# Moving the dense stretch of a weight conversion twelve steps earlier in a fused attention and expert kernel

## The chip, the cores and the metric

The kernel runs on one core of one Trainium2 chip. The metric is the device time of one execution in microseconds (us); lower is better. Engines are called by the profile's short names: PE (TensorE, matrix products; PEld is its weight load), DVE (VectorE), ACT (ScalarE), POOL (GpSimd) and SP (SyncE, which here only issues DMAs, in order).

## The reference

Three stages follow each other on 4 batches of 576 tokens. The kernel gets the inputs of the first two in 64-bit words, so weights have to be turned into 32-bit numbers on the chip.

```python
# 1: attention, 32 heads (4 batches x 8) of 576 x 64, with a decay bias from a running sum of s
cum = np.cumsum(np.maximum(s, 0.0), axis=-1)
bias = -(cum[:, :, :, None] - cum[:, :, None, :])
scores = np.where(causal, -1e9, scale * (q @ k^T) + np.minimum(bias, 0.0))
x = softmax(scores) @ v                       # heads joined: 4 x 576 x 512
# 2: token mixing of rank 32, and a feed-forward net 512 -> 2048 -> 512
u = x + ((x^T @ U) @ V)^T
y = u + np.maximum(u @ w_ch1, 0.0) @ w_ch2
# 3: four single-head attentions on y, the best two per token mixed by a gate
```

## The kernel before, in words

**Steps.** The first attention is written as a loop of steps `i`, five per head (one per block of query rows), 160 for 32 heads. A head pair `p` (two heads) takes ten steps, from step 10 x p. Instructions stand in each engine's queue in the order in which the loop writes them; no scheduler moves them. A step writes: the products `qk` of step i on PE (L361, L362), transposes `t` of the step ten before (L402, L405), the row minimum on DVE (L372), the exponential of step i-1 on ACT (L379), copies of the transposes out of PSUM, at a head's end the scaling of its rows on POOL (L390), a share of the product with V (`pv`, L429), and then what `fillers(i)` adds.

**Fillers.** `fillers(i)` adds, in this order: the preparation of the next pair (`prep_steps`: POOL and DVE split q and k into a high and a low part, and DMAs of L626 place them in the tiles `L`, `R`, `HI`, five pieces spread over six steps that end six steps before the pair starts); some slots of the weight conversion; and background work.

**Conversion.** One job converts a piece of 128 x 256 numbers. It is a load of 256 KB (`c_raw`, L186, issued on SP three jobs ahead), two passes on ACT (L116, L119), three on DVE (L122, L126, L130), and for the weight blocks f = 0, 1 and 2 a rounded high part on ACT (`wh`, L197) and the rest on POOL (`wl`, L200). A block f is four jobs. 24 jobs are converted in this loop: one of U, three of V, and four for each of f = 0 to 4. The list `STREAM` deals a job's parts over six slots, overlapped with its neighbours', and a step takes one slot or two:

```python
for _ in range(CONVS[FAST[0] < i < FAST[1]][i % NT]):   # CONVS: 1 a step, or 2 in the dense stretch
    if i >= 4 and convs:
        convs.pop(0)()
for _ in range(BG[i % NT]):                             # BG = (1, 1, 0, 2, 1)
    background()
```

**Background.** Once a batch's attention is done, its token mixing (`mx`, `mt`, `mo`: L236, L248, L259) and then the first three blocks of its feed-forward net are queued as small tasks. The net of one batch is 14 tasks: for each of two chunks of 288 tokens three `hps` (L293, 12 products, one per block f = 0, 1, 2) and four `facc` (L307, 9 products). A task `hps` of block f is taken only when that block is converted:

```python
ffn = ffnq and full.get(ffnq[0][0]) == 2 * DM
if mixq and (turn[0] % 2 or not ffn) and not (mixq[0][1] and ffnq):
    mixq.pop(0)[0]()
elif ffn:
    ffnq.pop(0)[1]()
```

This happens for batches 0, 1 and 2 inside the loop. After the loop come the other blocks of the net (L1010, L1028) and the last stage.

Of the kernel before, what the change touches and what calls it, by code (L numbers as in the profile page):

```python
# [50 lines left out]

PLAIN = (((0, 0),), ((0, 1),), ((0, 2), (1, -2)), ((1, -1),), ((2, -3),), ((0, 3),), ((0, 4),))
STREAM = (((0, 0), (3, -3)), ((-1, 4),), ((0, 1),), ((0, 2), (1, -2)), ((1, -1),), ((0, 3),))
FAST = (40, 70)
RAWS = 4

ENGA = ('vaaaaa', 'aavaav')
# [101 lines left out]
def fused_kernel(ctx, tc, qk, v, s, u, vv, w12, wp, out):  # L159
# [524 lines left out]
    with ExitStack() as cx:  # L684
# [228 lines left out]
        def fillers(i):  # L913
# [8 lines left out]
            for x in todo.pop(i, ()):  # L922
                x()
            for _ in range(CONVS[FAST[0] < i < FAST[1]][i % NT]):
                if i >= 4 and convs:
# [471 lines left out]
```

## Time and profile before

| what | value |
|---|---|
| time, median of 3 runs | 842.06 us (840.68 to 843.66) |
| the profiled execution: time / span | 842.4 us / 840.6 us |
| PE, PEld busy | 95%, 88% of the span |
| DVE, ACT, POOL busy | 63%, 56%, 38% of the span |
| granted clock of TensorE | 1.00 |

A product's end is modelled in the trace and products overlap, so that a busy PE is not PE at its peak. The span runs from the first to the last instruction; the time lies 1.8 us above it.

### The profile page before, as it was taken

What the parts mean: (1) busy time and instruction counts of PE and PEld (TensorE: products, weight loads), DVE (VectorE), ACT (ScalarE), POOL (GpSimd) and SP (SyncE); (2) the same over time, 40 slices, a digit from 0 to 9 for tenths busy, and PEclk for the clock granted to TensorE, in tenths of its full rate; (3) what the DMA queues carried; (4) which work ended last, traced back from release to release, by engine and by line L of the source; (5) the groups of instructions that cost most, each with busy time, mean ns of one, the idle gap of its engine ahead of it and who ended that gap; (6) DMA issues with size and microseconds to landing.
All of it is one profiled execution on the core that took longest, in us unless ns stands there. A gap on an engine that the chain in (4) does not pass through costs nothing.

```text
span 840.6 us, 17207 instructions
## 1 busy us (share of the span) xinstructions
PE 799.4 (95%) x6028; PEld 740.3 (88%) x6028; DVE 526.0 (63%) x1559; ACT 473.8 (56%) x1406; POOL 322.0 (38%) x483
## 2 busy tenths in 40 slices
PE   3889999999999899999999999999999989999997
PEld 2767779889888799999999999999999989898875
DVE  7779987776775357646554764455456775756541
ACT  5779996666776444434444442443334566655662
POOL 5647664453452334223322432232343043322231
PEclk9999999999999999999999999999999999999999
DMA  7887785745741342112111221210000111111221
GB/s 212 216 228 191 212 219 159 202 127 144 190 117 44 106 146 61 51 27 51 51 51 34 69 64 38 52 39 26 1 1 9 36 33 40 48 52 39 76 66 62
DMA packets 37048, 75.44 MB, mean 90 GB/s; under 512 B 4712, under 2 KB 8296, under 8 KB 36932
## 3 DMA queue, kind: packets, MB, share of 16 engines
q1 hardware_dynamic: 36964, 74.36, 32.5%
q8 instruction: 48, 0.79, 0.4%
q14 instruction: 36, 0.29, 0.1%
HBM read 38.93 MB, written 8.55 MB: 56 GB/s over the span
## 4 chain that ended last, share of the span: by engine, by line
PE 79%; DVE 10%; ACT 5%; DMA 3%; issue 2%; SPq 0%; POOL 0%; ACTq 0%; POOLq 0%; DVEq 0%
PE hps L1010 21%; PE facc L1028 21%; PE pv L429 4%; PE qkp L1237 4%; PE facc L307 3%; PE pv L589 3%; PE ops L1264 3%; PE hps L293 3%; PE t L402 3%; PE t L560 2%; PE vps L1171 2%; PE qk L361 2%; PE qk L362 2%; PE t L405 1%; DVE P L372 1%
## 5 line engine op out<-in xcount | busy, mean ns | idle before, releaser
L277 POOL TENSOR_TENSOR ul<-uT,uh 128x288 fp32r<-128x288 f32 x117 | 94.5, 828 | 163.9 <-ACT uh L276 138.1
L1015 DVE SCALAR_TENSOR_TENSOR hl<-hps,hh 128x288 fp32r<-128x288 f32 x110 | 50.3, 457 | 150.1 <-ACT hh L1014 150.1
L390 POOL TENSOR_SCALAR P<-P,stat 64x64 f32<-64x64 f32 (+4 forms) x160 | 101.7, 651 | 104.3 <-DVE stat L385 44.6
L1014 ACT ACTIVATE hh<-hps 128x288 fp32r<-128x288 f32 x110 | 45.0, 409 | 147.9 <-PE hps L1010 147.7
L85 ACT ACTIVATE pt<-t 64x64 f32<-64x64 f32 (+5 forms) x272 | 89.5, 358 | 42.0 <-PE t L405 29.6
L1010 PE MATMUL hps<-uh,wl 128*128 128x288 f32 x376 | 111.2, 296 | 0.0
L1010 PE MATMUL hps<-ul,wh 128*128 128x288 f32 x376 | 111.1, 296 | 0.0
L1028 PE MATMUL facc<-hh,wh 128*128 128x288 f32 x376 | 111.1, 296 | 0.0
L1010 PE MATMUL hps<-uh,wh 128*128 128x288 f32 x376 | 111.0, 295 | 0.0
L1028 PE MATMUL facc<-hh,wl 128*128 128x288 f32 x376 | 110.9, 295 | 0.0
L1028 PE MATMUL facc<-hl,wh 128*128 128x288 f32 x376 | 110.8, 295 | 0.0
L379 ACT ACTIVATE P<-P,stat 64x64 f32<-64x64 f32 (+4 forms) x160 | 89.2, 558 | 23.2 <-DVE stat L372 21.2
L548 POOL TENSOR_SCALAR P<-P,stat,pt 128x128 f32<-128x128 f32 (+4 forms) x72 | 45.8, 653 | 118.1 <-DVE stat L543 54.1
L372 DVE CUSTOM_DVE_ANT_0 P<-qk,mask 64x64 f32<-64x64 f32 (+4 forms) x160 | 77.4, 484 | 13.7 <-PE t L405 8.7
L361 PE MATMUL qk<-R,L 128*128 128x64 f32 (+2 forms) x192 | 66.3, 349 | 18.3 <-DVE L L750 9.6
L200 POOL TENSOR_TENSOR wl<-c_a_w,wh 128x256 fp32r<-128x256 f32 x56 | 43.8, 784 | 73.2 <-ACT wh L197 70.6
L1010 PEld LDWEIGHTS hps<-uh,wl 128*128 128x128 f32 x376 | 70.9, 189 | 0.0
L1028 PEld LDWEIGHTS facc<-hh,wl 128*128 128x128 f32 x376 | 70.9, 188 | 0.0
L1010 PEld LDWEIGHTS hps<-ul,wh 128*128 128x128 f32 x376 | 70.8, 188 | 0.0
L1028 PEld LDWEIGHTS facc<-hl,wh 128*128 128x128 f32 x376 | 70.8, 188 | 0.0
L1028 PEld LDWEIGHTS facc<-hh,wh 128*128 128x128 f32 x376 | 70.6, 188 | 0.1
L1010 PEld LDWEIGHTS hps<-uh,wh 128*128 128x128 f32 x376 | 70.6, 188 | 0.0
(211 smaller groups left out, 2230.0 us busy)
## 6 DMA issues: line engine op xcount, KB each, us to landing
c_raw_w<-in_w_dram SPq DMA_DIRECT2D x64, 256.0 KB
uT<-in_qk_dram SPq DMA_DIRECT2D x15, 576.0 KB
L<-HI SPq DMA_DIRECT2D x28, 288.0 KB
V<-in_v_dram SPq DMA_DIRECT2D x16, 320.0 KB
R<-HI SPq DMA_DIRECT2D x14, 288.0 KB
R<-uT SPq DMA_DIRECT2D x14, 288.0 KB
L<-uT SPq DMA_DIRECT2D x14, 288.0 KB
aD<-stage SPq DMA_DIRECT2D x6, 576.0 KB
```

The costliest lines, as they stand in the source:

```text
L85: nc.scalar.activation(out=out, in_=in_, func=AF.Copy)
L200: eng.tensor_tensor(out=wl, in0=t, in1=wh.bitcast(F32), op=OP.subtract)
L277: eng.tensor_tensor(out=l_, in0=src, in1=h_.bitcast(F32), op=OP.subtract)
L361: nc.tensor.matmul(ps[:, bk, :w], lhsT=q1[:, rows], rhs=k1[:, c0:c0 + w], start=True, stop=False)
L372: nc.vector.tensor_tensor_reduce(out=po, in0=view, in1=mk, scale=-self.scale, scalar=3.0e38, op0=OP.add, op1=OP.min, accum_out=stat[P - M: ...
L379: nc.scalar.activation(out=po, in_=po, func=AF.Exp, scale=-1.0, bias=stat[P - M:, 0, t:t + 1], accum_out=stat[P - M:, 1, t:t + 1])
L390: nc.gpsimd.tensor_scalar(out=pv, in0=pv, scalar1=stat[r0:, 2, t:t + 1], scalar2=1.0 if gate is None else gate(t)[r0:], op0=OP.mult, op1=O ...
L548: nc.gpsimd.tensor_scalar(out=po, in0=po, scalar1=stat[:, 2, s:s + 1], scalar2=1.0 if gate is None else gate(t), op0=OP.mult, op1=OP.mult)
L1010: nc.tensor.matmul(ps, lhsT=w[:, 0, cs], rhs=x, start=i == 0, stop=i == 11)
L1014: nc.scalar.activation(out=hh, in_=ps, func=AF.Relu)
L1015: nc.vector.scalar_tensor_tensor(out=hl, in0=ps, scalar=0.0, in1=hh.bitcast(F32), op0=OP.max, op1=OP.subtract)
L1028: nc.tensor.matmul(accs[c][d], lhsT=w[:, 1, cs], rhs=x, start=f == fs[0] and i == 0, stop=f == fs[-1] and i == 2)
```

## The change

One line: the dense stretch, in which a step takes two conversion slots, goes from steps 41 to 69 to steps 29 to 65. It is 37 steps long in place of 29.

```diff
 PLAIN = (((0, 0),), ((0, 1),), ((0, 2), (1, -2)), ((1, -1),), ((2, -3),), ((0, 3),), ((0, 4),))
 STREAM = (((0, 0), (3, -3)), ((-1, 4),), ((0, 1),), ((0, 2), (1, -2)), ((1, -1),), ((0, 3),))
-FAST = (40, 70)
+FAST = (28, 66)
 RAWS = 4
```

Counted from the code: steps 29 to 40 take 12 slots more, steps 66 to 69 take 4 less, and the stream, which is 8 slots ahead from there, ends at step 111 in place of 119. The last part of a block's conversion moves from step 47 to 41 (f = 0), 59 to 53 (f = 1), 73 to 65 (f = 2), 97 to 89 (f = 3) and 119 to 111 (f = 4).

Three places show what moves. The first is DVE's queue in step 30 and after, where head 6 starts (`qk_0` is its first block, `c_a_w` a piece of weights). Before:

```order
L87 COPY pt_106<-t_0_623 64x2x64
L849 TENSOR_TENSOR V_81<-c_a_v_547,V_81 128x192
L372 ISA P_114,stat_108<-qk_1_641,mask 128x192
L372 ISA stat_108 128x1
L384 TENSOR_SCALAR stat_112<-stat_112 128x5
L385 RECIPROCAL stat_112<-stat_112 128x5
L667 TENSOR_TENSOR uT<-uT,HI 128x576
L126 TENSOR_SCALAR c_a_w_0_666<-pt_106 128x256
L372 ISA P_114,stat_108<-qk_2_668,mask 128x320
L372 ISA stat_108 128x1
L667 TENSOR_TENSOR uT<-uT,HI 128x576
L130 ISA c_a_w_0_666<-c_a_w_0_666,pt_105 128x512
```

The same place with the change:

```order
L87 COPY pt_106<-t_0_624 64x2x64
L126 TENSOR_SCALAR c_a_w_0_641<-pt_106 128x256
L130 ISA c_a_w_0_641<-c_a_w_0_641,pt_105 128x512
L372 ISA P_114,stat_108<-qk_1_645,mask 128x192
L372 ISA stat_108 128x1
L384 TENSOR_SCALAR stat_112<-stat_112 128x5
L385 RECIPROCAL stat_112<-stat_112 128x5
L667 TENSOR_TENSOR uT<-uT,HI 128x576
L372 ISA P_114,stat_108<-qk_2_675,mask 128x320
L372 ISA stat_108 128x1
L667 TENSOR_TENSOR uT<-uT,HI 128x576
L122 SCALAR_TENSOR_TENSOR pt_105<-pt_107,c_r_w_256_670 128x256
```

The passes of the first piece (L126, L130) stand one and two steps earlier, and the first pass of the second piece (L122) has come into the row. The second place is SP's queue, where the tiles of pair 4 are placed in steps 29 to 34, before:

```order
L626 DMA L_0_122<-HI 64x1152
L626 DMA L_0_119<-HI 64x1152
L626 DMA R_0_121<-HI 64x1152
L626 DMA R_0_121<-uT 64x2x576
L626 DMA L_0_119<-uT 64x2x576
L626 DMA L_0_122<-Cd 2x2x576
L626 DMA HI<-Cd 4x2x576
```

and with the change:

```order
L626 DMA L_0_122<-HI 64x1152
L626 DMA L_0_119<-HI 64x1152
L626 DMA R_0_121<-HI 64x1152
L186 DMA c_raw_w_0_690<-in_w_dram 128x256
L626 DMA R_0_121<-uT 64x2x576
L626 DMA L_0_119<-uT 64x2x576
L626 DMA L_0_122<-Cd 2x2x576
L626 DMA HI<-Cd 4x2x576
```

A load of weights now stands ahead of the last four of pair 4's seven DMAs. The third place is PE's queue in steps 66 to 68 (`qk_2` and `qk_3` are the blocks of steps 67 and 68, `t_2` a transpose). Before:

```order
L405 MATMUL t_1_1473<-ident,P_116 64x128
L361 MATMUL qk_2_1494<-R_0_121,L_0_119 128x320
L362 MATMUL qk_2_1494<-HI,L_0_122 128x320
L402 MATMUL t_2_1497<-ident,P_116 128x128 x3
L405 MATMUL t_2_1497<-ident,P_116 64x128
L361 MATMUL qk_3_1509<-R_0_121,L_0_119 128x448
```

and with the change:

```order
L293 MATMUL hps_2_1514<-uh_3_1388,wh_1213 128x288
L293 MATMUL hps_2_1514<-ul_3_1389,wh_1213 128x288
L293 MATMUL hps_2_1514<-uh_3_1388,wl_1214 128x288
L361 MATMUL qk_2_1531<-R_0_121,L_0_119 128x320
L362 MATMUL qk_2_1531<-HI,L_0_122 128x320
L402 MATMUL t_2_1534<-ident,P_116 128x128 x3
L405 MATMUL t_2_1534<-ident,P_116 64x128
L361 MATMUL qk_3_1545<-R_0_121,L_0_119 128x448
```

The 12 products of block f = 2 for the first chunk (three of them shown), which stood in step 73, stand in step 66. Read in the same way over the whole queue, batch 0's 14 tasks go from steps 64 to 95 to steps 64 to 83, and batch 1's from steps 106 to 128 to steps 104 to 123. From step 130 on the queues of PE are the same in both.

## Rows read from the trace of the kernel before

**Rows 1.** The page: the span, and each engine's busy time.

```profile
span 840.6 us, 17207 instructions
PE 799.4 (95%) x6028; PEld 740.3 (88%) x6028; DVE 526.0 (63%) x1559; ACT 473.8 (56%) x1406; POOL 322.0 (38%) x483
```

**Rows 2.** Two stretches after the loop: length, busy us of each engine, clock, DMA.

```profile
300.00:350.00 50.00, 50.00 (x377) 50.00 (x377) 34.44 (x81) 22.80 (x64) 18.98 (x24) 1.00 0.22 57
...
550.00:600.00 50.00, 50.00 (x378) 50.00 (x377) 26.57 (x62) 19.70 (x54) 14.26 (x20) 1.00 0.10 28
```

**Rows 3.** Stretches of ten steps, steps 30 to 39 first; PE, PEld, DVE, ACT, POOL.

```profile
48.50:64.10 15.60, 14.33 (x111) 11.45 (x111) 11.63 (x38) 11.09 (x39) 8.62 (x14) 1.00 0.76 214
64.10:77.60 13.50, 11.60 (x91) 8.91 (x91) 13.14 (x44) 12.25 (x43) 9.52 (x14) 1.00 0.77 199
77.60:93.80 16.20, 14.75 (x114) 11.48 (x111) 14.52 (x45) 15.38 (x51) 12.26 (x19) 1.00 0.85 243
93.80:109.60 15.80, 15.22 (x114) 12.09 (x115) 15.04 (x50) 14.34 (x49) 9.11 (x13) 1.00 0.68 170
109.60:127.00 17.40, 17.12 (x139) 14.81 (x137) 15.50 (x47) 15.80 (x53) 12.54 (x19) 1.00 0.78 208
127.00:145.70 18.70, 18.70 (x146) 16.89 (x145) 12.88 (x44) 12.39 (x41) 9.29 (x15) 1.00 0.63 177
145.70:162.30 16.60, 16.34 (x137) 14.52 (x136) 12.55 (x44) 11.60 (x37) 5.93 (x11) 1.00 0.73 190
162.30:180.60 18.30, 17.50 (x144) 15.65 (x141) 14.98 (x49) 14.56 (x49) 8.74 (x14) 1.00 0.57 156
180.60:200.30 19.70, 19.44 (x161) 17.89 (x161) 13.80 (x45) 13.46 (x43) 9.32 (x14) 1.00 0.51 139
200.30:217.40 17.10, 17.10 (x142) 15.53 (x142) 11.05 (x37) 10.57 (x35) 7.07 (x13) 1.00 0.59 161
217.40:231.70 14.30, 13.76 (x112) 11.29 (x111) 10.20 (x36) 10.57 (x35) 7.27 (x12) 1.00 0.70 186
231.70:251.40 19.70, 19.27 (x155) 17.51 (x154) 14.70 (x48) 14.79 (x49) 10.58 (x15) 1.00 0.44 113
```

**Rows 4.** PE's timeline at step 40: start, us, engine, line, operation.

```profile
64.07 0.30 PE L361 MATMUL qk<-R,L 128*128 128x64 f32 x1
```

**Rows 5.** The chain that ended last, 30 to 50 us: start, us, what.

```profile
29.92 4.91 DMA HI<-Cd
...
44.04 4.99 DMA HI<-Cd
```

**Rows 6.** Steps 29 to 40 as one stretch, with columns as in rows 3.

```profile
46.10:66.30 20.20, 17.47 (x133) 13.49 (x132) 14.87 (x49) 15.69 (x54) 10.39 (x16) 1.00 0.70 196
```

**Rows 7.** Conversion passes on DVE, 30 to 180 us: busy us, mean ns of one.

```profile
L122 DVE SCALAR_TENSOR_TENSOR pt<-pt,c_r_w 128x256 uint32<-128x256 uint32 x19 | 9.0, 475 | 0.1
...
L126 DVE TENSOR_SCALAR c_a_w<-pt 128x256 uint32<-128x256 uint32 x18 | 7.3, 404 | 0.1
L130 DVE CUSTOM_DVE_ANT_0 c_a_w<-c_a_w,pt 128x512 uint16<-128x512 uint16 x12 | 7.2, 600 | 0.3
```

**Rows 8.** The chain: one `hps` task, and two `facc` tasks.

```profile
172.27 1.62 PE hps L293 x12
...
247.37 2.38 PE facc L307 x18
```

**Rows 9.** SP's issues for pair 4: start, us, line, what.

```profile
52.90 0.78 SPq L626 DMA_DIRECT2D R<-HI  x1
...
57.91 0.52 SPq L626 DMA_DIRECT2D HI<-Cd  x1
```

**Rows 10.** The same passes one by one: ns min/median/max.

```profile
L122 DVE SCALAR_TENSOR_TENSOR pt<-pt,c_r_w x19: 383/425/744, 47.8 to 177.7; 128x256 uint32<-128x256 uint32 x19
...
L126 DVE TENSOR_SCALAR c_a_w<-pt x18: 252/291/860, 52.8 to 172.3; 128x256 uint32<-128x256 uint32 x18
...
L130 DVE CUSTOM_DVE_ANT_0 c_a_w<-c_a_w,pt x12: 415/553/850, 54.4 to 111.6; 128x512 uint16<-128x512 uint16 x12
```

## The prediction

> **What bounds the kernel now.** I read the page first. PE is called busy for 799.4 of 840.6 us [rows 1], so only the places where it is not can give anything. The busy time by stretches shows where they are: from about 290 us to the last stage PE and its weight load are both busy for 50.00 of 50 us [rows 2], and nothing done in the attention loop can shorten that. The change lies wholly in the loop, steps 29 to 129, so I cut that part of the trace into stretches of ten steps, one head pair each, at PE's first product of every tenth step [rows 3]; step 40 is the one shown [rows 4].
>
> The reader is to see two regimes there. In steps 40 to 69 DVE and ACT are busy for 91% to 97% of the time (13.14 of 13.50, 15.38 of 16.20, 15.04 of 15.80), while PE's weight load has 66% to 77%: the vector engines set the pace. From step 80 on PE does wherever net tasks stand: in steps 80 to 89 it is busy for all of the 18.70 us and DVE for 12.88.
>
> The chain of waits adds one thing for steps 10 to 30: it runs through two DMAs of 4.9 and 5.0 us that finish the tiles of pairs 2 and 3 [rows 5]. Both are issued before step 29, so the change leaves them alone.
>
> **A ruler made of the rows.** A net task costs PE 1.62 us (`hps`) or 2.38 / 2 = 1.2 us (`facc`) [rows 8], one batch 6 x 1.6 + 8 x 1.2 = 19.2 us. Let F be the PE time of the tasks in a ten-step stretch, counted from PE's queue. Before, from step 60 on, F is 3.2, 5.2, 7.2, 3.6, 6.0, 8.4, 4.8, 0, 8.4, and the stretches take 15.8, 17.4, 18.7, 16.6, 18.3, 19.7, 17.1, 14.3, 19.7 us [rows 3]. The line through the emptiest and the fullest, 14.3 + 0.643 F, misses no stretch by more than 0.6 us. So a microsecond of tasks costs 0.64 wherever it stands, and the rest is hidden under the attention.
>
> **The change part by part.**
>
> *Twelve more slots in steps 29 to 40.* Twelve slots are two jobs. On DVE a job is 0.475 + 0.404 + 0.600 = 1.48 us [rows 7], so 3.0 us are added to a stretch of 20.2 us in which DVE is busy for 14.87 and ACT for 15.69 [rows 6]. The idle 5.3 us of DVE could hold all of it: the lower bound is 0, the upper 3.0. The nearest rows are steps 50 to 59, which carry 20 slots and a batch's mixing and take 16.2 us, and steps 130 to 139, which carry the same kind of mixing and no slot and take 14.3: 1.9 / 20 = 0.095 us for a slot. I take 12 x 0.095 = **+1.1**.
>
> *Net tasks move forward.* Block f = 2 is ready at step 65, not 73, so no `hps` waits for it. F becomes, for the stretches from step 60 to 129, 8.4, 8.4, 2.4, 0, 8.4, 8.4, 2.4. The sum is 38.4 in both, so the line gives the same total: 7 x 14.3 + 0.643 x 38.4 = 124.8 us. But the trace has 123.6 (93.8 to 217.4): the spread order of before lies 1.2 below the line, whereas four of the new stretches are as full as the two that fix its upper end, and one as empty as the lower. I take **+1.2**. If the new order lies as far below the line as the old one, the term is 0, and if twice as far, -1.2, which I take as the lower end; the upper end is in the first rival.
>
> *Four slots less in steps 66 to 69.* That is where tasks now enter, and DVE is at 95%: 4 x 0.095 = **-0.4**; at full price -1.0.
>
> *Eight slots less in steps 112 to 119.* PE is busy for 19.44 of 19.70 us there and DVE for 13.80, so what DVE saves is slack: **0**. If PE were not the cover, it would be 8 x 0.095 = -0.8.
>
> *Loads.* The raw loads go forward with their jobs, some two more by step 40. One of 256 KB stands ahead of the last four DMAs of pair 4 on SP. At that stretch's 214 GB/s it is 1.2 us. Before, the last of them is issued at 57.91 [rows 9]; if it takes 5.0 us as in rows 5, it lands at 62.9, and step 40 starts at 64.07 [rows 4]. The delay just fits: **0**, and +1.2 if it doesn't.
>
> Sum: 1.1 + 1.2 - 0.4 = +1.9. The profiled execution, 842.4 us, becomes 844.3. It lies 0.3 above the median of the runs, 842.06, so the median becomes **844.0**, which is +0.2%. About 0.3%, 2.5 us, is what a measurement of this kernel can tell from no change, so this counts as the same, on the slow side.
>
> **The rivals.**
>
> *Slower: the conversion loses its cover in steps 84 to 103.* Batch 0's tasks are over at step 83 and batch 1's begin at step 104, yet one slot a step goes on. If 20 light steps pay 0.095 for a slot as steps 50 to 59 do, that is +1.9: 845.9. For it: the light stretches would run at the pace of DVE. Against it: steps 90 to 99 carry ten slots with F = 3.6 and lie on the line that steps 130 to 149, without a slot, fix. It decides from 0.6 us on, since 844.6 is the border.
>
> *Slower: DVE pays more than the mean in steps 29 to 40.* The same pass takes 252 or 860 ns, another 383 or 744, the third 415 or 850 [rows 10]; at the longest two jobs are 4.9 us. All on the path, that is 3.8 over the 1.1 that I took: 847.8. POOL, whose scaling of rows runs beside them, is busy for half of that stretch [rows 6], against 76% in steps 50 to 59, where the price came from, so I hold it unlikely. The Trainium skill (SBUF — State Buffer, "Who interferes with whom") says that VectorE and GpSimd lock a shared port pair and the later one blocks; this spread agrees with it, and no row shows which engine waited.
>
> *Slower: the load in front of pair 4.* +1.2 at step 40: 845.2.
>
> *Faster: PE has room in steps 60 to 79.* There the weight load is busy for 12.09 of 15.80 and 14.81 of 17.40 us, and for 15.65 of 18.30 in steps 100 to 109. If tasks filled that room, the three stretches would take 12.09 + 5.2 = 17.3, 14.81 + 3.2 = 18.0 and 15.65 + 2.4 = 18.05 in place of 19.7 each: -5.8, 838.2. Against it: the stretches that are full already, steps 80, 110 and 140 on, keep 1.8 to 2.2 us outside the weight load (18.70 - 16.89, 19.70 - 17.89, 19.70 - 17.51), and with 1.8 the sums come back to 19.1 or more. The Trainium skill (Perfetto Trace Analysis, "Identifying the Most-Contended Engine") says that headroom on TensorE is to be judged by the weight load's busy share and not by the product's; that rule stands behind this rival, and the three full stretches are why it gets a small chance.
>
> *It does nothing.* If attention hides the twelve slots and the light stretches are as far below the line as steps 60 to 69 were, the sum is near 0, 842: this is the lower part of my forecast, and no case of its own.
>
> **How the numbers follow.** The forecast holds all that ends within 2.5 us of 842.06, that is 839.5 to 844.6, most of it above 842: 0.47. Uncovered conversion: 0.24. DVE's longest passes: 0.08. The late load: 0.06. PE's room: 0.15. Faster is the last, 0.15; same the first, 0.47; slower the other three, 0.38. The range is 839.0 to 848.0: it holds the forecast, the three slow cases and the weaker half of the fast one.
>
> **What would show it.** In the profile after, steps 29 to 40 should take 20.2 + 1.1 = 21.3 us, with DVE busy for nearly 3 us more. Steps 60 to 69 and 70 to 79 should take near 19.7 each in place of 15.8 and 17.4, and steps 80 to 89 and 90 to 99 near 15.9 and 14.3 in place of 18.7 and 16.6. Steps 60 to 129 together should take 124 to 125 us. From step 130 to the end the length should be as before. The prediction is wrong if steps 60 to 79 take 36 us or less (PE's room), if steps 80 to 103 run at 1.6 us a step or more (uncovered conversion), or if step 40 waits for a DMA.

## The result and the profile after

The changed kernel takes 854.42 us (median of 4 runs, 852.11 to 854.84) against 842.86 us of the kernel before beside it (840.68 to 844.29). The ratio is 1.0129, with a 95% interval from 1.0113 to 1.0145: 11 us slower. The forecast was the same time within noise, 844.0 us, and its range ended at 848.0.

The page of the changed kernel has almost the same busy times as before [rows 1]; the span is 11.8 us longer, and PE is busy for 6.5 us more with the same 6028 products.

```profile
span 852.4 us, 17211 instructions
PE 805.9 (95%) x6028; PEld 743.0 (87%) x6028; DVE 525.9 (62%) x1559; ACT 474.5 (56%) x1406; POOL 319.6 (37%) x483
```

So the time is lost in places, not by more work. The stretches of ten steps answer to [rows 3], from step 40 on: length, busy time of PE, PEld, DVE, ACT and POOL, granted clock, DMA share and rate.

```profile
63.50:79.10 15.60, 13.29 (x92) 10.09 (x91) 14.87 (x46) 13.74 (x47) 10.83 (x16) 0.89 0.80 217
79.10:95.30 16.20, 14.78 (x114) 11.50 (x111) 13.63 (x44) 14.57 (x48) 11.04 (x18) 1.00 0.87 244
95.30:115.60 20.30, 20.18 (x155) 17.53 (x155) 18.07 (x55) 17.45 (x58) 13.57 (x19) 1.00 0.54 147
115.60:135.40 19.80, 19.80 (x160) 17.85 (x160) 13.25 (x45) 13.20 (x44) 6.93 (x13) 1.00 0.65 181
135.40:151.90 16.50, 14.88 (x112) 12.16 (x110) 12.58 (x42) 10.87 (x37) 6.79 (x11) 1.00 0.58 148
151.90:169.10 17.20, 15.78 (x110) 12.50 (x111) 10.75 (x37) 11.45 (x38) 7.22 (x13) 0.90 0.71 206
169.10:189.30 20.20, 19.56 (x155) 17.47 (x154) 16.78 (x55) 15.84 (x52) 10.78 (x16) 1.00 0.45 122
189.30:209.20 19.90, 19.44 (x162) 17.90 (x161) 12.14 (x40) 12.28 (x40) 7.76 (x14) 1.00 0.56 152
209.20:226.40 17.20, 15.18 (x124) 12.90 (x122) 10.82 (x38) 10.90 (x36) 6.04 (x11) 1.00 0.50 127
226.40:243.20 16.80, 15.67 (x110) 12.34 (x111) 9.54 (x33) 9.54 (x32) 6.86 (x12) 0.90 0.63 176
```

Steps 60 to 79 take 20.3 and 19.8 us, as the ruler said (19.7). The return did not come: steps 80, 90 and 120 on take 16.5, 17.2 and 17.2 in place of the forecast 15.9, 14.3 and 15.9. Steps 130 to 139, whose queue on PE is unchanged, take 16.8 in place of 14.3. The column of the clock is below 1.00 in three rows, and it was nowhere before.

PE's timeline where step 90 begins, and then where step 130 does (start, us, what, in brackets the idle time before and what ended it):

```profile
151.93 0.27 PE L361 MATMUL qk<-R,L 128*128 128x64 f32 x1 [1.49 <-DMA L<-uT]
152.89 0.39 PE L362 MATMUL qk<-HI,L 68*128 68x64 f32 x1 [0.69 <-DMA HI<-Cd]
...
226.43 0.30 PE L361 MATMUL qk<-R,L 128*128 128x64 f32 x1 [2.01 <-DMA L<-uT]
227.27 0.27 PE L362 MATMUL qk<-HI,L 68*128 68x64 f32 x1 [0.54 <-DMA L<-Cd]
```

Both pair starts wait for the DMAs that place their tiles, 2.2 and 2.6 us. The DMA queue of SP shows why. Its issues around step 84:

```profile
145.29 0.57 SPq L824 DMA_DIRECT2D aD<-stage  x1
145.91 0.63 SPq L626 DMA_DIRECT2D R<-uT  x1
146.60 1.08 SPq L626 DMA_DIRECT2D L<-uT  x1
147.72 1.14 SPq L626 DMA_DIRECT2D L<-Cd  x1
148.96 0.97 SPq L626 DMA_DIRECT2D HI<-Cd  x1
```

The waits of that queue, 140 to 147 us (who waited for whom: us, times, longest), and the chain of waits at the same place:

```profile
SPq L824 <- DVE stage L822: 6.1, 1, 6.1
```

```profile
143.58 1.20 PE facc L307 x9
...
144.80 0.47 DVE stage L822
...
148.96 3.80 DMA HI<-Cd
152.76 0.14 issue
152.89 0.39 PE qk L362
```

The reader is to see one chain (pieces of it are left out above). The last net task of a chunk (`facc`) ends, DVE adds it into `stage`, and only then can SP issue the store of the chunk (L824), for which it has stood 6.1 us. Behind it stand the four DMAs of pair 9. The data of the first of them had been ready since DVE's `uT<-uT,HI` ended:

```profile
142.82 0.75 DVE L667 TENSOR_TENSOR uT<-uT,HI 128x576 fp32r<-128x576 f32 x1
```

That is 143.57, and the DMA was issued at 145.91: 2.3 us late. Around step 124 SP waits 7.8 us in the same way. After each wait PE runs at its lower level. Three stretches are at that level. The first of them, at 74 us, follows no DMA wait: PE had stood still for 0.77 and 0.89 us there, until ACT's copies `pt` ended. Below them stand the three stretches just ahead, in the same order:

```profile
74.30:77.70 3.40, 3.19 (x13) 2.38 (x14) 3.33 (x13) 3.34 (x13) 1.99 (x4) 0.50 0.80 244
152.80:156.20 3.40, 3.31 (x15) 2.40 (x17) 2.17 (x10) 1.64 (x8) 1.34 (x2) 0.51 0.66 246
227.90:231.30 3.40, 3.40 (x22) 2.16 (x22) 2.56 (x9) 1.47 (x6) 1.90 (x3) 0.50 0.30 116
```

```profile
70.90:74.30 3.40, 1.74 (x13) 1.29 (x12) 3.27 (x12) 3.29 (x12) 3.21 (x4) 1.00 0.75 201
149.50:152.80 3.30, 1.21 (x9) 0.84 (x7) 2.54 (x8) 2.71 (x10) 2.12 (x4) 1.00 0.75 211
224.50:227.90 3.40, 0.93 (x7) 0.85 (x8) 0.77 (x2) 1.50 (x5) 0.58 (x1) 1.00 0.72 218
```

PE had been busy for 1.74, 1.21 and 0.93 us just ahead of each fall, and the granted clock then is 0.50 or 0.51, that is 1.2 in place of 2.4 GHz. The Trainium skill (TensorE: Matmul & The Clock Gate, "Part 1: The HAM clock gate") says that idleness throttles this engine's clock to half and activity releases it; the trace agrees on the two levels, though PE had not been idle throughout ahead of any of the falls.

### The profile page after: what moved, and what is told of

Same layout as the page of the kernel before. It is cut to its first block, busy times and chain, and to the rows that moved or that the text cites. A ratio compares the mean times of both kernels' runs of the same rounds, so it can differ in the third digit from the quotient of the medians.

```text
span 852.4 us, 17211 instructions
## 1 busy us (share of the span) xinstructions
PE 805.9 (95%) x6028; PEld 743.0 (87%) x6028; DVE 525.9 (62%) x1559; ACT 474.5 (56%) x1406; POOL 319.6 (37%) x483
## 4 chain that ended last, share of the span: by engine, by line
PE 77%; DVE 9%; ACT 5%; DMA 3%; issue 2%; SPq 1%; POOL 1%; ACTq 0%; POOLq 0%; DVEq 0%
PE hps L1010 21%; PE facc L1028 20%; PE pv L429 5%; PE qkp L1237 4%; PE facc L307 3%; PE pv L589 3%; PE ops L1264 3%; PE hps L293 3%; PE t L402 3%; PE t L560 2%; PE vps L1171 2%; DVE P L372 2%; PE qk L362 1%; PE qk L361 1%; SPq L626 1%
## 5 line engine op out<-in xcount | busy, mean ns | idle before, releaser
L390 POOL TENSOR_SCALAR P<-P,stat 64x64 f32<-64x64 f32 (+4 forms) x160 | 99.5, 636 | 119.9 <-DVE stat L385 63.6
```

The costliest lines, as they stand in the source:

```text
L390: nc.gpsimd.tensor_scalar(out=pv, in0=pv, scalar1=stat[r0:, 2, t:t + 1], scalar2=1.0 if gate is None else gate(t)[r0:], op0=OP.mult, op1=O ...
```

## The experiments

My theory after the result was the chain above: the moved net tasks carry a store, and in SP's queue the store stands ahead of the DMAs of pairs 9 and 13. Rivals were the early conversion itself, the crowding of net tasks in steps 64 to 83, and the lighter conversion load at the end. Times are medians; each ratio is to the kernel before, run beside it, over all runs of both, and so it is not the quotient of two medians.

| run | time us | ratio | 95% interval |
|---|---|---|---|
| e1, dense stretch early, net tasks as before | 842.31 | 0.9992 | 0.9982 to 1.0001 |
| e2, conversion as changed, net tasks held | 843.64 | 1.0015 | 1.0005 to 1.0025 |
| e3, changed, stores behind | 846.24 | 1.0044 | 1.0027 to 1.0062 |
| e4, changed, products in the wait | 850.39 | 1.0093 | 1.0076 to 1.0109 |
| e5, before, stores behind | 842.85 | 0.9996 | 0.9987 to 1.0005 |
| e6, e1 with stores behind | 842.67 | 0.9991 | 0.9979 to 1.0003 |
| e7, before, last piece later | 843.66 | 1.0008 | 0.9996 to 1.0020 |
| e8, changed, last piece ahead of the store | 848.08 | 1.0056 | 1.0036 to 1.0075 |
| e9, e3, last piece later | 846.68 | 1.0050 | 1.0034 to 1.0066 |
| e10, e3, second chunk held | 845.67 | 1.0027 | 1.0017 to 1.0038 |

**e1: the dense stretch moved, the net tasks not.**

```diff
-FAST = (28, 66)
+FAST = (28, 58)
```

> The dense stretch goes from step 29 to step 57, so that conversion is 12 slots ahead in steps 41 to 57 and level with the kernel before from step 70 on; the order on PE is that of the kernel before. If the early conversion itself costs (all of my +1.1 us or more), the ratio to before is 1.001 to 1.004. If the loss comes from the moved net tasks or from what stands behind them on SP, the ratio is 0.999 to 1.002 and steps 80 to 135 take what they took before.

0.9992: moved as a whole, the dense stretch costs nothing that these runs can tell. Steps 29 to 40 in e1, and then steps 40 to 49 (columns as above):

```profile
46.00:66.40 20.40, 17.72 (x138) 13.44 (x134) 17.19 (x51) 17.52 (x59) 12.19 (x18) 1.00 0.84 221
63.70:78.50 14.80, 11.94 (x91) 8.95 (x90) 14.41 (x46) 12.80 (x45) 9.73 (x15) 1.00 0.78 213
```

DVE is busy for 17.19 us where it was for 14.87 [rows 6], and the stretch takes 20.4 in place of 20.2. The 5.3 us in which DVE had been idle took the slots there. But steps 40 to 49 take 14.8 us in place of 13.5, with DVE busy for 14.41. What makes e1 level is that its steps 60 to 69 have ten slots less than before and take 14.8 us in place of 15.8. The changed kernel, which is dense up to step 65, has the first of the two and little of the second.

**e2: the conversion moved, the net tasks not.** The lines that keep the step in `step[0]` are left out.

```diff
-ffn = ffnq and full.get(ffnq[0][0]) == 2 * DM
+ffn = ffnq and full.get(ffnq[0][0]) == 2 * DM and (ffnq[0][0] < 2 or step[0] >= 73)
```

> Conversion as in the changed kernel, but the first net task of block 2 is held until step 73, so that all net tasks and their stores stand where they stood before. If the moved tasks (by their crowding, or by their stores on SP) carry the loss, the ratio to before is 0.998 to 1.003. If the moved conversion carries it, by the lighter load in steps 112 to 119 or the heavier one in 29 to 40, it stays at 1.008 or more.

1.0015: with the net tasks back in their steps, nearly all of the loss is gone. The moved tasks carry it. The moved conversion keeps a little: the interval lies clear of 1, and steps 40 to 49 take 14.6 us in e2's trace in place of 13.5.

**e3: the stores behind the pair's DMAs.** The list `stores`, the helper `flush` and its last call behind the loop are left out.

```diff
 if d == KD - 1:
-    nc.sync.dma_start(out=aD[:, :, c * CH:c * CH + CH], in_=stage["t"])
+    stores.append((aD[:, :, c * CH:c * CH + CH], stage["t"]))
...
 for x in todo.pop(i, ()):
     x()
+if r == 5:
+    flush()                # issues what is in stores
```

> The changed kernel, with each store of a finished chunk issued at the next step with remainder 5 of 10, behind the last piece of the pair's preparation, not ahead of it. If the store at the head of SP's queue delays pairs 9 and 13, the waits of 2.2 and 2.6 us at steps 90 and 130 fall under 0.5 us, the clock stays at its higher level there, and the time falls by 6 to 9 us, to a ratio of 1.003 to 1.007. If the crowding of net tasks carries the loss, the ratio stays above 1.010.

1.0044, so of the 1.29% that were lost 0.85% come back. Steps 80, 90, 120 and 130 on in e3:

```profile
135.40:150.30 14.90, 14.74 (x112) 12.21 (x111) 10.98 (x38) 9.68 (x34) 5.48 (x10) 1.00 0.63 145
150.30:165.70 15.40, 14.46 (x114) 11.59 (x112) 12.09 (x41) 12.73 (x42) 9.09 (x15) 1.00 0.86 249
...
205.80:220.80 15.00, 14.96 (x124) 12.96 (x123) 9.88 (x38) 9.16 (x31) 5.25 (x10) 1.00 0.53 121
220.80:235.60 14.80, 14.24 (x113) 11.51 (x111) 10.79 (x36) 11.41 (x38) 8.32 (x14) 1.00 0.73 190
```

They fall by 1.6, 1.8, 2.2 and 2.0 us, and the clock is 1.00 in all of them. On SP the first of pair 9's four DMAs leaves at once, and the store (L833 in this kernel) follows them:

```profile
143.60 0.62 SPq L626 DMA_DIRECT2D R<-uT  x1
...
145.75 1.03 SPq L626 DMA_DIRECT2D HI<-Cd  x1
...
147.47 0.61 SPq L833 DMA_DIRECT2D aD<-stage  x1
```

**e4: work for PE in the wait.** The added products compute nothing that is used.

```diff
 for _ in range(BG[i % NT]):
     background()
+if i in (89, 129):
+    ps = bank(f"dm_{i}")[:, :HALF]
+    for x in range(12):
+        nc.tensor.matmul(ps, lhsT=V4[:, 0, 0:P], rhs=V4[:, 0, 0:HALF], start=x == 0, stop=x == 11)
```

> The changed kernel with twelve idle products of 288 columns (1.6 us, result unused) added to PE at steps 89 and 129, ahead of the two waits. If the lower clock behind the waits is a cost of its own, it stays at 2.4 GHz after steps 90 and 130, steps 130 to 134 fall from 10.3 to about 8 us, and the time falls by 3 to 5 us. If the drop is only a sign, the time rises by 0 to 3 us.

1.0093: 24 useless products, 1.8 us of PE for each twelve in the trace, make the kernel faster than the changed one, by 0.36% or some 3 us. Steps 90 and 130 on in e4:

```profile
151.10:166.80 15.70, 14.18 (x111) 11.48 (x111) 10.74 (x37) 11.44 (x38) 7.78 (x13) 1.00 0.80 226
...
223.90:239.10 15.20, 14.12 (x111) 11.56 (x112) 10.01 (x33) 9.62 (x34) 7.36 (x12) 1.00 0.64 160
```

The clock stays at 1.00, and these stretches take 15.7 and 15.2 us in place of 17.2 and 16.8: 1.5 and 1.6 us are the price of the lower clock. The mean granted clock of the four runs is 0.997 to 0.999, that of the changed kernel's four 0.992 to 0.996. Steps 130 to 134 take 8.7 us, less far down than the 8 that I had expected. The stretches ahead of them, in which the waits lie, stay at 16.5 and 17.0.

**e5 and e6: the stores behind, without the moved net tasks.** e3's edit with `FAST = (40, 70)` and with `FAST = (28, 58)`.

> The kernel before with its stores of finished chunks issued behind the pair's preparation. There the net tasks end later, so only the stores of steps 81 and 128 stand ahead of a pair's DMAs, and no pair start waits for them for long: ratio 0.997 to 1.001. If the stores always cost, as much as in the changed kernel, it is 0.994 or less.

> Dense stretch from step 29 to 57 and stores behind the preparation: the two edits that cost nothing by themselves. Ratio to before 0.996 to 1.001. Below 0.997 it would beat both kernels.

0.9996 and 0.9991: no difference that these runs can tell. A store ahead of a pair's DMAs is not dear by itself. The kernel before had one at step 81, just ahead of the same four DMAs:

```profile
134.07 0.58 SPq L824 DMA_DIRECT2D aD<-stage  x1
135.35 0.62 SPq L626 DMA_DIRECT2D R<-uT  x1
...
137.76 0.96 SPq L626 DMA_DIRECT2D HI<-Cd  x1
```

DVE ended the data of the first of the four at 135.33, and it left at 135.35: the store had gone in time, and nothing stood waiting behind it. Neither run, nor e1, beats the kernel before clearly.

**e8: the same two queue neighbours, swapped the other way.**

```diff
-for x in PREP if p > 1 else PREP1:
+for x in (PREP[:4] + (3,) if p in (9, 13) else PREP) if p > 1 else PREP1:
```

> The changed kernel with the last piece of preparation of pairs 9 and 13 written one step earlier, so that it stands ahead of the store in SP's queue and the store stays where it was. If the order of these two is the cause, the waits at steps 90 and 130 go as in the run with the store behind, and the ratio to before is 1.002 to 1.007. If the store's own traffic or place is the cause, it stays at 1.010 or more.

1.0056: the store stays where it was, the four DMAs go ahead of it, and most of the loss is gone. Its interval overlaps that of e3, and in its trace steps 80, 90, 120 and 130 on take 14.8, 15.4, 15.0 and 14.8 us, within 0.1 us of e3's; what e3's trace does not have is a fall of the clock at 76 us. So the order of the two is the cause, not the store's traffic.

**e7 and e9: the last piece later.** The edit of e8 with a 6 in place of the 3, in the kernel before (e7) and in e3 (e9, with the stores at remainder 7).

> The kernel before with the last piece of preparation of pairs 9 and 13 (four DMAs) issued two steps later, at steps 86 and 126 in place of 84 and 124, some 2.5 to 3.5 us. If a late issue alone makes the loss, whatever the net tasks do, it costs 2 to 5 us a pair start or a ratio of 1.004 to 1.010. If the loss needs the emptied steps 84 to 89 and 124 to 129, which shorten the lead, it is hidden here: 0.999 to 1.003.

> The run with the stores behind, with the last piece of preparation of pairs 9 and 13 issued two steps later, at steps 86 and 126, and the stores at remainder 7. In the kernel before the same lateness cost nothing. If the emptied steps 84 to 89 and 124 to 129 are what makes it dear, pair starts 90 and 130 wait again for DMAs, 1.5 to 3 us each, with a lower clock behind one or both, and the ratio to before rises from 1.0044 to 1.008 to 1.014. If lateness is harmless here too and only the store mattered, it stays at 1.003 to 1.006.

The two were made to tell whether lateness alone makes the loss. e9 doesn't tell. SP issues as soon as the data are ready and nothing ahead of it waits, so that a place two steps later in its queue was no later issue: `HI<-Cd` for pair 9 leaves at 145.01 in e9 and at 145.75 in e3, in both 10.3 us after step 80 begins.

e7 tells more. The later place let three loads go ahead of the four DMAs. `HI<-Cd` leaves at 138.36, 12.0 us after the start of step 80 (before: 137.76, 10.8 us), but the landings in the trace, put to the DMAs by their order, have `L<-uT` arrive only at 145.94. Step 90 begins at 146.03, after 0.75 us in which PE stood still and for which the profile itself names no wait. The stretches ahead of steps 90 and 130 take 19.7 and 17.9 us in place of 18.7 and 17.1. So lateness is not free in the old order of the net tasks, but most of it is hidden there; how much is worked out below.

**e10: the place of net tasks without their stores in the way.** This is e3 with the edit below; the lines that count the tasks and the step in `took` are left out.

```diff
-ffn = ffnq and full.get(ffnq[0][0]) == 2 * DM
+ffn = ffnq and full.get(ffnq[0][0]) == 2 * DM and not (took[0] == 7 and took[1] < 83)
```

> The run with the stores behind, with the seven net tasks of batch 0's second chunk held until step 83: net time by stretches of ten from step 60 is then 8.4, 1.2, 9.6, 0, 8.4, 8.4, 2.4. If the straight ruler holds, the place of a task does not matter and the ratio to before is 1.003 to 1.006, as without the hold; steps 70 to 79 take about 15.1 us and steps 80 to 89 about 20.5. If the crowded steps 65 to 74, with conversion beside them, carry what is left, it falls to 1.002 or less.

1.0027, between the two expectations, and its interval overlaps that of e3: unclear. Its stretches say more. With net time of 8.4, 1.2, 9.6 and 0 us, steps 60, 70, 80 and 90 on take

```profile
95.90:116.30 20.40, 20.22 (x154) 17.56 (x155) 18.18 (x55) 17.45 (x58) 13.65 (x20) 1.00 0.57 153
116.30:132.00 15.70, 15.18 (x121) 12.53 (x120) 11.98 (x40) 11.35 (x37) 6.76 (x12) 1.00 0.74 193
132.00:151.20 19.20, 19.20 (x152) 17.66 (x151) 14.08 (x45) 12.57 (x43) 7.59 (x12) 1.00 0.64 182
151.20:166.00 14.80, 14.07 (x113) 11.44 (x112) 11.15 (x38) 11.70 (x39) 7.73 (x13) 1.00 0.72 181
```

that is 70.1 us, against 70.4 in e3 with 8.4, 8.4, 2.4 and 0. Once nothing waits on SP, it does not matter for the sum where the tasks stand, within what these traces can tell. For single stretches the line is less good than before: it gave 15.1 and 20.5 us for steps 70 to 79 and 80 to 89.

## Why the prediction was wrong

- **Twelve slots in steps 29 to 40, +1.1.** The size was right, the place was not. Steps 29 to 40 themselves paid 0.2 (e1), where 21.3 us were forecast: DVE's idle time took the slots. But steps 40 to 49, for which the sum had nothing, take 14.5 to 14.8 us in place of 13.5 in every trace with the early stretch and the clock at 1.00 there, 1.0 to 1.3 more. Why the price falls there stays open.
- **Net tasks move forward, +1.2, and four slots less, -0.4.** This was the step that failed, and not mainly by its arithmetic on PE. With the stores out of the way (e3) steps 60 to 129 take 20.3 + 19.8 + 14.9 + 15.4 + 20.2 + 19.9 + 15.0 = 125.5 us, +1.9 over the 123.6 before, where I had 0.8; so 1.1 us of the loss is the size of this term. What I left out is that a moved task moves all it issues. The last `facc` of a chunk issues a store on SP, and I followed SP's queue only to step 40, for the raw loads. At step 83 the store came to stand one step ahead of the last four DMAs of pair 9, and at step 123 of pair 13's.
- **No word on lead.** In the kernel before, `HI<-Cd` for pair 9 was issued at 137.76 and step 90 began at 145.7, a lead of 8 us; in the changed kernel's chain the transfer takes 3.8. In e3, with steps 84 to 89 emptied of net tasks, it is issued at 145.75 and step 90 begins at 150.31: 4.6 us. The faster steps had eaten the lead. In the changed kernel, whose step 80 begins at the same 135.4, it leaves at 148.96, 3.2 us later (2.3 behind the store, and 0.9 because the issues of the two DMAs of `L` took longer), and that is more than the 0.8 that was left. That the emptied steps are needed for the loss follows from e7. Counted from the start of step 80, the last of the four DMAs has landed after 14.4 us in the kernel before, 17.3 in the changed one and 19.6 in e7, by the landings in the traces. Steps 80 to 89 take 18.7 us in the old order and 14.9 in the new one (e3) when nothing waits. So the changed kernel waits for a transfer that lands earlier than the one that costs e7 0.9 us, and in the old order 17.3 us would have been covered.
- **No word on the clock.** Each wait brought half clock behind it. From the changed kernel to e4 steps 80 to 139 lose 3.3 us (17.2 + 17.2 + 16.8 to 15.7 + 17.0 + 15.2, the others equal), and from e4 to e3 4.3 (16.5 + 15.7 + 17.0 + 15.2 to 14.9 + 15.4 + 15.0 + 14.8). So the two stores cost 7.6 us, 4.3 in waits and 3.3 in clock.
- **The account.** Of 11.8 us between the two profiled executions, 7.6 are the stores, 1.9 the crowded tasks, 2.1 the stretch of steps 40 to 49 (15.6 us in place of 13.5) and 0.5 steps 130 to 139 (14.8 in e3 in place of 14.3); what is left, ahead of step 40 and behind step 139, takes 0.3 off. In e1, e3 and e4 steps 40 to 49 take 14.5 to 14.8 with the clock at 1.00, so about 1 us of the 2.1 is conversion and 1 us the fall of the clock at 74 us, which the traces of e1, e3 and e4 don't have.
- **The rivals.** Uncovered conversion in steps 84 to 103: its sign came true, since steps 80 to 99 ran at 1.7 us a step (16.5 and 17.2), but from another cause. e3, with the same conversion, has 14.9 and 15.4, together 30.3, where the line without this rival gives 30.2. DVE's longest passes: wrong, by e1's 20.4 us for steps 29 to 40. A late DMA at step 40: the right mechanism at the wrong place; step 40 did not wait. PE's room in steps 60 to 79: wrong, 20.3 and 19.8 us.

What stays open: why steps 40 to 49 pay for the early slots, the 1.1 us by which the crowded tasks cost more than the sum had, and why the clock fell at 74 us. That fall is in the traces of the changed kernel and of e8 (at 76 us) and not in the others with the same queues there. A trace is one execution, and such falls come and go: e2, e3, e5 and e10 have 3.4 us at half clock from 35 to 36 us on, which the kernel before does not have, though its queues and those of e5 are the same up to there. One of the six runs of e3 took 850.65 us at a mean clock of 0.992, and no trace shows where.

## What to carry to other kernels

When work moves in a hand-written order, list what it issues on every queue, and for each in-order queue ask what comes to stand behind an instruction that waits. A DMA that waits for a result goes behind those whose data are ready: that was worth 0.85% here, and nothing in the kernel whose steps left enough lead. Making a stretch faster shortens the lead of all that was prepared a fixed number of steps ahead of it, and an idle gap on TensorE can be paid a second time in its clock, as it was here.

## What the hardware showed that I had not expected

After a gap in which PE was busy for 1.21 of 3.30 or 0.93 of 3.40 us, it ran 3.4 us at half clock, which cost 1.5 to 1.6 us more: two waits of 2.2 and 2.6 us cost 7.6 in all. Twelve useless products (1.8 us of PE) ahead of each wait kept the clock up and made the kernel some 3 us faster.
